# A linear-attention and gated MLP kernel on one core: the weight guard as a later check, the state product in four TensorE tiles, eight masks moved from VectorE

## The chip, the cores and the metric

The kernel runs on one core of one Trainium2 chip. The metric is device time of one execution in microseconds, the median of several runs; before the change it is 392.2 us (three runs, 391.81 to 392.32).

## What is computed

For 4 batches and 8 heads a recurrence over 768 steps runs on states of 48 by 48; its output, with the heads side by side, goes through a token-shifted, gated MLP (384 to 1024 to 384):

```python
f = 1.0 / (1.0 + np.exp(-f_logit))
for t in range(S):
    state = f[:, :, t, :, None] * state + np.einsum('bhd,bhe->bhde', k[:, :, t], v[:, :, t])
    y[:, :, t] = np.einsum('bhd,bhde->bhe', q[:, :, t], state)
...
xk = mu_k * x + (1.0 - mu_k) * x_prev      # x: y with heads joined; x_prev: one step earlier
xr = mu_r * x + (1.0 - mu_r) * x_prev
k = np.maximum(xk @ w_k, 0.0)
v = k * k @ w_v
r = 1.0 / (1.0 + np.exp(-(xr @ w_r)))
return (r * v).astype(np.float32)
```

The weights arrive as 64-bit floats, as pairs of 32-bit words, and are made into 32-bit floats on the chip.

## The kernel before

**Attention.** The work is cut into 24 chunks of 128 steps (six to a batch). Two heads share a tile, head a in partitions 0 to 47 and head b in 64 to 111, and four such pairs make the 8 heads. For chunk i the names of the steps are: b (scan of the gates on VectorE, L203), ln and rb (logarithm and exponential on ScalarE), q, n and k (products on VectorE, L213, L233, L225 and L229), kr (two products on GpSimd, L221 and L222), SC (scores, TensorE, L274, into the PSUM tiles pss0 for heads a and pss1 for heads b), ma and mb (the two masked copies to SBUF, L300), TR and kt (transposed k, L259, and its copy, L262), ZQ (the state's product with q, L284), VV (scores times v, L284), PP (new state contribution, L315, into the PSUM tile pp), zs and z (state update on VectorE, L247 and L249), and y (two ScalarE copies from the PSUM tile py into x and stage, L330). SC uses TensorE as four independent 64 by 64 tiles. ZQ uses it as two: heads a in rows and columns 0 to 63, heads b in the other half. VV uses all 128 rows and alternates between the two column halves.

**MLP.** Three chunks make a unit of 384 steps; there are 8 units. Six small DMAs (spread, L385) move heads 6 and 7 from stage into x's free partitions. The mix makes d (three differences, L395), xm (six, L404), and each xm's high part xh and low part xl (L412 or L413, and GpSimd's L419). Every full-size product is the sum of three matmuls of high and low parts (L427): F (eight tiles with w_k), R (three with w_r), W (three output tiles of two halves each with w_v; W0.01 is the second half of unit 0's first tile). Between F and W stand r, h, kk (ScalarE) and k2l (GpSimd, L465).

**Weights.** Each of 18 pieces (wk0 to wk7 of 384 columns, wr0 to wr3 of 288, wv0 to wv5 of 512) goes through A (absolute value on ScalarE, L543), M (maximum with 2^-15, L546), S (shift, L548), T and X (combining the words, L551 and L554, all VectorE), H (cast to the high part, ScalarE, L557) and L (the rest, GpSimd, L561). M guards S against weights of very small size. The six wv pieces pass through two buffers called words.

**Order.** A planner (Plan.schedule, L73) simulates the queues with costs and due times written into each `pl.add`, and emits every engine's instructions in the order that it finds; each engine then runs its own list in order and waits on semaphores. SP issues all DMAs, in order. If any gate product falls below a bound (flag, L608), the slow path `general` runs at the end; it doesn't run here.

Of the kernel before, what the change touches and what calls it, by code (L numbers as in the profile page):

```python
# [47 lines left out]


class Plan:  # L50
# [22 lines left out]
    def schedule(self, trace=None):  # L73
        free = dict.fromkeys("PVAGQ", 0.0)
        wire = 0.0
# [79 lines left out]
class Rwkv:  # L155


    def __init__(self, nc=None, tc=None):
# [17 lines left out]
    def add_attention(self, pl, i):  # L176
# [104 lines left out]
        first = [None, None]  # L281

        def ymm(g2, j, lhs, rhs, stop):
            m = nc.tensor.matmul(  # L284
                self.py[64 * g2 : 64 * g2 + lhs.shape[1], j], lhs, rhs, start=first[g2] is None, stop=stop,
                skip_group_check=True,
            )
            first[g2] = first[g2] or m

        def zq():  # L290
            for j in range(NP):
                for g2 in (0, 1):
                    ymm(g2, j, self.z_t[i % 2][HALF[g2], j], q()[HALF[g2], j], False)

        if cs > 0:
            pl.add(f"ZQ{i}", at, ("P", 0.87, 0, zq), after=I("z") + I("q") + I("y", i - 1) + I("SC"))
        for g2, m in enumerate("ab"):
# [26 lines left out]
        def y_out(e):  # L324

            for r in (slice(0, D), slice(64, 64 + D)) if cs == 0 else (slice(0, P),):
                for o, i_ in ((self.b("x", u)[r, :, 1 + t0 : 1 + t0 + C], self.py[r, 0:3]),
                              (self.b("stage", u)[r, t0 : t0 + C], self.py[r, 3])):
                    if e is nc.scalar:
                        e.activation(o, i_, AF.Copy, scale=-1.0)  # L330
# [4 lines left out]
        pl.add(f"y{i}", at, ("A", us, 0, lambda: y_out(nc.scalar)), ("V", us, 0, lambda: y_out(nc.vector)),
               after=I("VV"), **({"takes" if c == 0 else "uses": [("x", u), ("stage", u)]}))

    def add_unit(self, pl, u):
# [42 lines left out]
    def spread(self, x, stage, j):  # L381

        for g2 in (0, 1):
            r = 64 * g2
            self.nc.sync.dma_start(x[r + 48 : r + 64, j, 1:], stage[r + 16 * j : r + 16 * j + 16, :])  # L385

    def add_mix(self, pl, u, k0, dst, alone=False):
# [46 lines left out]
        for f in range(NF):  # L434
# [36 lines left out]
        for t in range(UC):  # L471
# [343 lines left out]
```

## Time and profile before

| | |
|---|---|
| runs | 392.20, 392.32, 391.81 us |
| profiled execution | 392.84 us; span from first to last instruction 391.1 us |
| TensorE matmul (PE) busy | 339.2 us, 87% of the span, 3241 instructions |
| VectorE (DVE) busy | 231.2 us, 59%, 429 instructions |
| ScalarE (ACT) busy | 237.1 us, 61%, 458 instructions |
| GpSimd (POOL) busy | 184.6 us, 47%, 212 instructions |
| data moved by DMA | 34.17 MB, mean 87 GB/s |
| mean granted TensorE clock | 0.977 of full speed |

A row of a timeline is start, duration, engine, line, operation, tiles (buffer numbers left out), count, and in brackets the idle time of the engine before it with what ended it. A group row ends with busy time, mean nanoseconds of one, and idle time before the group. PE is the matmul part of TensorE and PEld its weight loads. One fp32 matmul of the attention shows as two PE instructions. Rows of the chain of waits are start, duration and what ran.

### The profile page before, as it was taken

To read this page: it belongs to the slowest core of one execution; us is meant where nothing else is said; L and a number is where in the kernel's file an instruction comes from. 1 tells how busy PE (TensorE), PEld (TensorE's weight loads), DVE (VectorE), ACT (ScalarE), POOL (GpSimd) and SP (SyncE) were. 2 spreads that over 40 slices of the span, in tenths; PEclk is the share of its full clock that TensorE was granted. 3 is DMA by queue.
4 is the path that set the end of the run, shared out by engine and by line. 5 is a ranking of instruction groups with operands and counts; after the bars stand their busy time and mean duration, and the time that the engine had idled before them with its cause. 6 is when DMAs were issued, how large, how long until landed. Compare 5 with 4: busy or idle time off the path is not lost.

```text
span 391.1 us, 8274 instructions
## 1 busy us (share of the span) xinstructions
PE 339.2 (87%) x3241; PEld 314.9 (81%) x3241; DVE 231.2 (59%) x429; ACT 237.1 (61%) x458; POOL 184.6 (47%) x212
## 2 busy tenths in 40 slices
PE   0077227699999999999999999999999999999994
PEld 0066126689898998999899989999899989999993
DVE  6989699998797588318851688049822731161001
ACT  4773348868478765747675655856584436565830
POOL 1451377764667564534574364618361613334600
PEclk9999859999999999999999999999999999999999
DMA  7999611343550243421321123032301100011001
GB/s 250 402 372 233 150 54 55 108 99 84 140 118 5 59 99 108 117 60 38 103 62 33 45 83 102 2 75 76 91 20 30 47 23 2 1 37 40 3 21 47
DMA packets 17918, 34.17 MB, mean 87 GB/s; under 512 B 2928, under 2 KB 13040, under 8 KB 17872
## 3 DMA queue, kind: packets, MB, share of 16 engines
q1 hardware_dynamic: 17872, 33.57, 30.1%
q8 instruction: 27, 0.44, 0.5%
q14 instruction: 19, 0.16, 0.1%
HBM read 27.66 MB, written 4.72 MB: 83 GB/s over the span
## 4 chain that ended last, share of the span: by engine, by line
PE 78%; DVE 9%; DMA 8%; ACT 1%; issue 1%; SPq 1%; DVEq 0%
PE pm L427 59%; PE py L284 10%; PE pss L274 5%; DMA v<-in_vt 3%; PE pm L259 2%; DMA f<-in_zt 2%; DMA x<-stage 2%; PE pp L315 2%; DVE pm L548 1%; DVE pm L551 1%; DVE pm L546 1%; DVE xm L404 1%; DVE pm L395 1%; DMA x<-in_wr 1%; DVE words L554 1%
## 5 line engine op out<-in xcount | busy, mean ns | idle before, releaser
L427 PE MATMUL pm<-xh,wk 128*128 128x384 f32 x384 | 107.5, 350 | 19.1 <-DVE words_k2h L554 13.5
L427 PE MATMUL pm<-wv,k2h 128*128 128x384 f32 x384 | 99.8, 341 | 0.4 <-DVE xm L404 0.4
L465 POOL TENSOR_TENSOR k2l<-kk,k2h 128x384 fp32r<-128x384 f32 x64 | 65.0, 1018 | 60.3 <-ACT kk L459 38.3
L427 PEld LDWEIGHTS pm<-xh,wk 128*128 128x128 f32 x384 | 71.6, 192 | 22.8 <-issue 14.1
L419 POOL TENSOR_TENSOR xl<-xm,xh 128x384 fp32r<-128x384 f32 x48 | 53.3, 1125 | 50.3 <-DVE xh L413 39.7
L427 PEld LDWEIGHTS pm<-wv,k2h 128*128 128x128 f32 x384 | 69.0, 188 | 1.8 <-issue 0.9
L427 PE MATMUL pm<-xl,wk 128*128 128x384 f32 x192 | 65.9, 343 | 0.0
L427 PE MATMUL pm<-wv,k2l 128*128 128x384 f32 x192 | 64.8, 338 | 0.0
L300 DVE TENSOR_TENSOR ss<-pss,cst_sb 128x512 f32<-128x512 f32 x48 | 30.8, 683 | 53.5 <-PE pss L274 53.3
L450 ACT ACTIVATE r<-pm 128x384 f32<-128x384 f32 x64 | 31.4, 490 | 32.2 <-PE pm L427 27.9
L274 PE MATMUL pss<-qk 64*64 64x128 f32 (+1 forms) x768 | 23.1, 258 | 22.1 <-DVE qk L225 22.1
L274 PEld LDWEIGHTS pss<-qk 64*64 64x64 f32 x768 | 19.6, 139 | 27.4 <-DVE qk L225 22.1
L427 PE MATMUL pm<-wr,xh 128*128 128x384 f32 x144 | 38.5, 349 | 0.0
L427 PEld LDWEIGHTS pm<-xl,wk 128*128 128x128 f32 x192 | 36.8, 192 | 0.0
L395 DVE TENSOR_TENSOR pm<-x 128x384 f32<-128x384 f32 x24 | 18.2, 757 | 30.9 <-DMA x<-stage 30.7
L427 PEld LDWEIGHTS pm<-wv,k2l 128*128 128x128 f32 x192 | 36.1, 188 | 0.0
L455 ACT ACTIVATE k2h<-r 128x384 fp32r<-128x384 f32 x64 | 33.6, 525 | 2.0
L517 DVE TENSOR_TENSOR o<-pm,lg 128x384 f32<-128x384 f32 x24 | 13.2, 551 | 35.7 <-PE pm L427 35.7
L221 POOL TENSOR_TENSOR qk<-qk,rb 128x256 f32<-128x256 f32 x24 | 22.5, 937 | 24.5 <-ACT rb L211 14.2
L203 DVE TENSOR_TENSOR_SCAN pm<-f,low 128x512 f32<-128x512 f32 x24 | 32.8, 1365 | 0.0
L412 ACT CAST xh<-xm 128x384 fp32r<-128x384 f32 x36 | 18.2, 514 | 20.2 <-DVE xm L404 20.0
L459 ACT ACTIVATE kk<-r 128x384 f32<-128x384 f32 x59 | 30.0, 509 | 0.1
(81 smaller groups left out, 529.2 us busy)
## 6 DMA issues: line engine op xcount, KB each, us to landing
qk<-in_qkt SPq DMA_DIRECT2D x40, 192.0 KB, 3.4
v<-in_vt SPq DMA_DIRECT2D x24, 192.0 KB, 2.5
out<-o SPq DMA_DIRECT2D x24, 192.0 KB, 1.9
words<-in_wv SPq DMA_DIRECT2D x6, 512.0 KB, 3.7
f<-in_zt SPq DMA_DIRECT2D x10, 288.0 KB, 4.9
qk<-in_qkt SPq DMA_DIRECT2D x4, 512.0 KB, 8.8
f<-in_zt SPq DMA_DIRECT2D x2, 768.0 KB, 8.4
words_k2h<-in_wk SPq DMA_DIRECT2D x4, 384.0 KB, 9.4
```

What stands on the lines that cost most here:

```text
L203: pl.add(f"b{i}", ga, ("V", 1.25, 1, lambda: nc.vector.tensor_tensor_scan(b().rearrange(FL), f().rearrange(FL), self.low.rearrange(FL), 1. ...
L221: e.tensor_tensor(k()[:, ::2], k()[:, ::2], rb()[:, ::2], op=ALU.mult)
L274: nc.tensor.matmul(self.pss[g2][HALF[h ^ j], j0 + j, 64 * h :], k()[HALF[g2], j0 + j, HALF[h ^ j]], q()[HALF[g2], j0 + j, 64 * h :], start ...
L284: m = nc.tensor.matmul(self.py[64 * g2 : 64 * g2 + lhs.shape[1], j], lhs, rhs, start=first[g2] is None, stop=stop, skip_group_check=True,)
L300: nc.vector.tensor_tensor(s4, p4, self.mask.unsqueeze(1).to_broadcast([P, 2, 2, C]), op=ALU.mult)
L395: pl.add(f"d{u}.{j}", pr, ("V", 0.56, 1, lambda j=j: nc.vector.tensor_tensor(pm("d", u, j)[:, :UT], x()[:, j, 1:], x()[:, j, :UT], op=ALU. ...
L419: e.tensor_tensor(lo(), xm(), hi().bitcast(F32), op=ALU.subtract)
L427: nc.tensor.matmul(ps, lhs(a, j), rhs(bb, j), start=ends[0] and i == 0, stop=ends[1] and i == len(pr) - 1)
L450: pl.add(f"r{u}.{f}", kf, ("A", 0.5, 0, lambda r=r, ps=ps: nc.scalar.activation(r(), ps(), AF.Relu)), ("V", 0.56, 0, lambda r=r, ps=ps: nc ...
L455: pl.add(f"h{u}.{f}", kf, ("A", 0.53, 0, lambda r=r, hi=hi: nc.scalar.activation(hi(), r(), AF.Square)), after=[f"r{u}.{f}"], **kw)
L459: ("A", 0.53, 0, lambda r=r, kk=kk: nc.scalar.activation(kk(), r(), AF.Square)),
L465: e.tensor_tensor(lo(), kk(), hi().bitcast(F32), op=ALU.subtract)
```

## The change

Three things are changed together, and with them the planner's numbers and so the order.

1. *Guard as a check.* A and M go from all 18 pieces; S now reads the loaded words. In their place `add_check` loads all weights a second time, in 15 pieces through the two words buffers, and reduces each to its least absolute value (VectorE). The least of all joins the flag. The slow path makes the weights again, with the guard.
2. *State product in four tiles.* ZQ and VV write to two PSUM tiles: even pairs to py, odd pairs to pz, which is the second half of the bank that holds pp. For odd pairs the column halves are swapped, so that ZQ's four matmuls of two pairs use the four 64 by 64 tiles in turn. VV's column halves follow each other as 0 1 1 0 0 1 1 0. y becomes four copies (six in the first chunk of a batch), since the swapped pair must be put back, and is placed after PP.
3. *Masks.* For chunks 0 to 7 mb is a plain ScalarE copy, and GpSimd multiplies by the mask in SBUF (mg); VV waits for it.

```diff
+CHECK = (2.0, 0.2)
+AWAY = [(i, 1) for i in range(8)]
...
             if e == "Q":
-                done = wire = max(wire, start + 1.5) + us
-                free[e] = start + 0.06
+
+                for _ in range(port):
+                    start = max(start, under[-8])
+                    wire = max(wire, start + 1.6) + us / port
+                    under.append(wire + 0.3)
+                    start += 0.45
+                done, free[e] = wire + 0.3, start
...
         def ymm(g2, j, lhs, rhs, stop):
-            m = nc.tensor.matmul(
-                self.py[64 * g2 : 64 * g2 + lhs.shape[1], j], lhs, rhs, start=first[g2] is None, stop=stop,
-                skip_group_check=True,
-            )
+
+            h = g2 ^ j % 2
+            to = (self.pz if j % 2 else self.py)[64 * h : 64 * h + lhs.shape[1], j // 2]
+            m = nc.tensor.matmul(to, lhs, rhs, start=(h, j % 2) not in first, stop=stop, skip_group_check=True)
...
+            if (i, g2) in AWAY:
+                ss = lambda: self.b("ss", (i, 1))
+
+                def by_mask():
+                    s4 = ss().rearrange("p (a b) c -> p a b c", b=2)
+                    nc.gpsimd.tensor_tensor(
+                        s4, s4, self.mask.unsqueeze(1).to_broadcast([P, 2, 2, C]), op=ALU.mult)
+
+                pl.add(f"m{m}{i}", at, ("A", 0.59, 0, lambda: nc.scalar.copy(ss(), self.pss[1])), after=I("SC"),
+                       takes=[("ss", (i, g2))])
+                pl.add(f"mg{i}", at, ("G", 1.35, 0, by_mask), after=I("mb"), uses=[("ss", (i, g2))])
...
-                for o, i_ in ((self.b("x", u)[r, :, 1 + t0 : 1 + t0 + C], self.py[r, 0:3]),
-                              (self.b("stage", u)[r, t0 : t0 + C], self.py[r, 3])):
+                for o, i_ in ((x[r, 0:3:2], self.py[r]), (stage[r], self.pz[r, 1])):
...
+            for r in (0, 64):
+                o, i_ = x[r : r + D, 1], self.pz[64 - r : 64 - r + D, 0]
...
-               after=I("VV"), **({"takes" if c == 0 else "uses": [("x", u), ("stage", u)]}))
+               after=I("VV") + I("PP"), **({"takes" if c == 0 else "uses": [("x", u), ("stage", u)]}))
...
-            pl.add(f"{name}A{p}", place, ("A", us(0.00104, 0.14), 0, lambda: nc.scalar.activation(
-                t(), high().bitcast(F32), AF.Abs)), after=[f"{name}{p}"], takes=[t_key], uses=[home])
             dve = us(0.00104, 0.15)
-            pl.add(f"{name}M{p}", place, ("V", dve, 0, lambda: nc.vector.tensor_scalar(
-                t(), t(), 2.0**-15, None, op0=ALU.max)), after=[f"{name}A{p}"], uses=[t_key])
...
+            pl.add(f"c{p}", CHECK[0] + CHECK[1] * p, ("Q", n * P * 8 / 380e3, 1, lambda v=v, w=w, c=c: nc.sync.dma_start(
+                v(), w.rearrange("p a b t -> p (a b) t")[:, c])), takes=[("words", ("c", p))])
+            pl.add(f"cm{p}", CHECK[0] + CHECK[1] * p + 1, ("V", 0.00104 * n + 0.15, 0, lambda v=v, p=p: nc.vector.tensor_reduce(
+                self.least[:, p : p + 1], v()[..., 1].bitcast(F32), axis=mybir.AxisListType.X, op=ALU.min,
+                apply_absolute_value=True)), uses=[("words", ("c", p))])
...
+            nc.vector.scalar_tensor_tensor(
+                self.flag, m()[:, 1:2], 2.0**-15, m()[:, 0:1], op0=ALU.is_lt, op1=ALU.max)
...
-    k.py = pm.tile([P, NP, C], F32, name="py")
+
+    k.py = pm.tile([P, 512], F32, name="py")[:, : 2 * C].rearrange("p (a c) -> p a c", a=2)
     k.pp = pm.tile([P, 512], F32, name="pp")
+    k.pz = k.pp[:, 256:].rearrange("p (a c) -> p a c", a=2)
```

What it does to the order is seen at three places. The first is VectorE's list (DVE) where unit 0's mix begins. L395 is d, L404 is xm, and L546, L548, L551, L554 are M, S, T, X of a piece. Before:

```order
L554 SCALAR_TENSOR_TENSOR words_k2l_126<-words_k2l_126,pm_88 128x3x128
L395 TENSOR_TENSOR pm_88<-x_101 128x384
L404 SCALAR_TENSOR_TENSOR xm_105<-pm_88,mu_sb,x_101 128x384
L546 TENSOR_SCALAR pm_86<-pm_86 128x384
L548 TENSOR_SCALAR pm_86<-pm_86 128x384
L551 SCALAR_TENSOR_TENSOR pm_86<-words_k2l_126,pm_86 128x384
L554 SCALAR_TENSOR_TENSOR words_k2l_126<-words_k2l_126,pm_86 128x3x128
L395 TENSOR_TENSOR pm_86<-x_101 128x384
```

The same place now, with d at L428, xm at L437 and S, T, X at L578, L587, L590:

```order
L590 SCALAR_TENSOR_TENSOR words_k2l_127<-words_k2l_127,pm_90 128x3x128
L578 TENSOR_SCALAR pm_89<-words_k2h_128 128x384
L428 TENSOR_TENSOR pm_87<-x_102 128x384
L437 SCALAR_TENSOR_TENSOR xm_106<-pm_87,mu_sb,x_102 128x384
L428 TENSOR_TENSOR pm_88<-x_102 128x384
L437 SCALAR_TENSOR_TENSOR xm_107<-pm_88,mu_sb,x_102 128x384
L428 TENSOR_TENSOR pm_90<-x_102 128x384
L437 SCALAR_TENSOR_TENSOR xm_108<-pm_90,mu_sb,x_102 128x384
L437 SCALAR_TENSOR_TENSOR xm_109<-pm_87,mu_sb,x_102 128x384
```

Before, piece wk3 stands between the first and the second d; now wk3 and the shift of wk4 stand ahead of the mix, and the nine instructions of the mix follow each other.

The second place is TensorE's list (PE) where unit 0's W meets chunk 5: k2l_666 ends W0.01, pss is SC, z is ZQ, and k2h_539 begins the second output tile. Before:

```order
L427 MATMUL pm_87<-wv_79,k2l_666 128x384
L274 MATMUL pss_81<-qk_65 64x128
L274 MATMUL pss_82<-qk_65 64x128
...
L274 MATMUL pss_82<-qk_65 64x64
L284 MATMUL py<-qk_65,z_71 64x128 x8
L427 MATMUL pm_86<-wv_79,k2h_539 128x384
```

Now, where k2l_572 ends the first half W0.00, L272 is TR, and k2h_619 begins W0.01:

```order
L460 MATMUL pm_90<-wv_79,k2l_572 128x384
L287 MATMUL pss_81<-qk_65 64x128
...
L300 MATMUL py<-qk_65,z_71 64x128 x2
L300 MATMUL pp<-qk_65,z_71 64x128 x2
...
L272 MATMUL pm_89<-cst_sb,qk_66 128x128 x4
L287 MATMUL pss_81<-qk_66 64x128
...
L460 MATMUL pm_90<-wv_79,k2h_619 128x384
```

SC and ZQ of chunk 5 and TR and SC of chunk 6 moved from behind W0.01 to ahead of it, and ZQ's eight matmuls go to py and to pp's bank by turns.

The third place is VectorE's list at the state update after chunk 1, zs and z, with what each instruction waits for. Before:

```order
L554 SCALAR_TENSOR_TENSOR words_k2h_125<-words_k2h_125,pm_86 128x3x128 [waits DVE_49]
L247 TENSOR_TENSOR pp<-pp,z_71 128x192 [waits PE_49]
L249 TENSOR_TENSOR z_70<-pp,g 128x4x48 [waits DVE_49]
L300 TENSOR_TENSOR ss_93<-pss_81,cst_sb 128x512 [waits PE_49]
L300 TENSOR_TENSOR ss_92<-pss_82,cst_sb 128x512 [waits PE_49]
```

Now:

```order
L242 SCALAR_TENSOR_TENSOR qk_67<-pm_90,qk_67 128x2x64
L260 TENSOR_TENSOR pp<-pp,z_71 128x192 [waits PE_49,Activation_49]
L262 TENSOR_TENSOR z_70<-pp,g 128x4x48 [waits DVE_49]
L578 TENSOR_SCALAR pm_87<-words_k2h_126 128x384 [waits DMAHW2_49]
L587 SCALAR_TENSOR_TENSOR pm_87<-words_k2h_126,pm_87 128x384 [waits DVE_49]
L315 TENSOR_TENSOR ss_95<-pss_81,cst_sb 128x512 [waits PE_49]
```

zs now waits for ScalarE too: for the last copy of y of the chunk before, which reads the bank that pp lies in. Of the two masks only that of heads a is left in VectorE's list.

More of the change, by code (lines that the diff above doesn't have):

```diff
@@ L155 @@
 class Rwkv:
+    wk = wr = wv = None
     def __init__(self, nc=None, tc=None):
@@ L356, in add_unit @@
         else:
-            pl.add(f"f{u}", ga - 0.4 if u >= NFB else -1.5 + 0.1 * u, ("Q", 1.8, 0, load), after=gates)
+            pl.add(f"f{u}", ga - 0.4 if u >= NFB else -1.5 + 0.1 * u, ("Q", 2.07 if u < NFB else 1.55, 1 if u < NFB else 2, load), after=gates)
             if u < NFB:
@@ L365, in add_unit @@
         for j in range(KJ):
-            pl.add(f"sp{u}.{j}", u - PREP - 0.1, ("Q", 0.2, 0, lambda j=j: self.spread(x(), s(), j)), after=ys, uses=[("x", u), ("stage", u)])
+            pl.add(f"sp{u}.{j}", u - PREP - 0.1, ("Q", 0.2, 2, lambda j=j: self.spread(x(), s(), j)), after=ys, uses=[("x", u), ("stage", u)])
         if u % NU == 0:
@@ L440, in ff @@
                 mm3(ps(), lambda a, j: wk_p()[a][:, j, f * P : f * P + P], lambda a, j: sp(0)[a][:, j], range(KJ))
-            pl.add(f"F{u}.{f}", kf, ("P", 1.57, 0, ff), after=chain + [f"xl{u}.0{j}" for j in range(KJ)]
+            pl.add(f"F{u}.{f}", kf, ("P", 1.58, 0, ff), after=chain + [f"xl{u}.0{j}" for j in range(KJ)]
                    + ([] if alone else [f"wkL{f}"]),
@@ L476, in rp @@
                 mm3(ps(), lambda a, j: sp(1)[a][:, j, t * P : t * P + P], lambda a, j: wr_p()[a][:, j], range(KJ))
-            pl.add(f"R{u}.{t}", kr, ("P", 1.57, 0, rp), after=chain + [f"xl{u}.1{j}" for j in range(KJ)]
+            pl.add(f"R{u}.{t}", kr, ("P", 1.58, 0, rp), after=chain + [f"xl{u}.1{j}" for j in range(KJ)]
                    + ([] if alone else [f"wrL{p}" for p in range(4)]),
@@ L592, in add_words, with add_check @@
                   *(lambda c=c, a=a: self.w["wv"][a].rearrange("p a b -> p (a b)")[:, c] for a in (0, 1)), True)
+    def add_check(self, pl):
+        nc = self.nc
+        pieces = [(w, slice(c, c + m)) for w, n, m in ((self.wk, KJ * DFF, 512), (self.wv, NF * DM, 512), (self.wr, KJ * DM, DM))
+                  for c in range(0, n, m)]
+        for p, (w, c) in enumerate(pieces):
+            n = c.stop - c.start
+            v = lambda p=p, n=n: self.b("words", ("c", p))[:, : 2 * n].bitcast(I32).rearrange("p (n t) -> p n t", t=2)
+            pl.add(f"c{p}", CHECK[0] + CHECK[1] * p, ("Q", n * P * 8 / 380e3, 1, lambda v=v, w=w, c=c: nc.sync.dma_start(
[3 more added lines that the diff above has]
+                apply_absolute_value=True)), uses=[("words", ("c", p))])
+        return [f"cm{p}" for p in range(len(pieces))]
@@ L613, in add_start @@
         at = U - 1
[L614 to L620 removed]
+        pl.add("lo", at, ("V", 0.4, 0, least), after=[f"bl{N - 1}"] + self.add_check(pl), takes=[("xm", "lo")])
+        pl.add("lot", at, ("P", 0.2, 0, turn), takes=[("pm", "lo")], uses=[("xm", "lo")])
+        pl.add("lom", at, ("V", 0.6, 0, flag), uses=[("pm", "lo"), ("xm", "lo")])
+        pl.add("strong", at + 0.3, ("Q", 0.0, 0, load), after=["lom"])
     def rows(self, first):
```

139 lines of the change are left out of this document (84 added, 55 removed).

## Prediction

> **What bounds the kernel now.** I read the page first, then busy time by windows, the chain of waits, and the timelines of PE and DVE in the start.
>
> ```profile
> span 391.1 us, 8274 instructions
> PE   0077227699999999999999999999999999999994
> DVE  6989699998797588318851688049822731161001
> ```
>
> PE is full from the ninth slice to the end (a slice is 9.8 us); before that DVE is. By windows (PE, PEld, DVE, ACT, POOL busy, clock, DMA share, GB/s):
>
> ```profile
> 50.00:60.00 10.00, 3.64 (x11) 3.18 (x12) 9.64 (x16) 4.11 (x8) 6.18 (x6) 0.53 0.18 52
> 60.00:70.00 10.00, 7.58 (x41) 6.65 (x40) 9.54 (x17) 9.52 (x22) 8.45 (x8) 1.00 0.30 79
> ...
> 160.00:180.00 20.00, 20.00 (x162) 19.14 (x161) 5.07 (x11) 14.30 (x26) 7.80 (x9) 1.00 0.30 69
> 180.00:200.00 20.00, 20.00 (x227) 18.41 (x226) 17.86 (x32) 11.87 (x27) 12.66 (x15) 1.00 0.28 83
> ```
>
> So there are two regimes. From about 45 to 85 us the DVE queue (weight words, first mix) feeds PE; afterwards PE's own work is the time, and DVE has slack in alternate windows. The joints between them, from the timelines of PE, DVE and SP:
>
> ```profile
> 56.33 0.66 PE L427 MATMUL pm<-xh,wk 128*128 128x384 f32 x1 [13.13 <-DVE words_k2h L554]
> ...
> 90.34 0.52 PE L427 MATMUL pm<-wv,k2h 128*128 128x384 f32 x2
> ```
>
> ```profile
> 38.94 4.67 SPq L385 DMA_DIRECT2D x<-stage  x6
> ```
>
> ```profile
> 44.62 0.57 DVE L395 TENSOR_TENSOR pm<-x 128x384 f32<-128x384 f32 x1 [2.82 <-DMA x<-stage]
> ...
> 45.76 0.56 DVE L546 TENSOR_SCALAR pm<-pm 128x384 f32<-128x384 f32 x1
> ```
>
> The rows are PE's first full-size matmul F and the one at 90.34, SP's issue of the first unit's spread, and the first difference d0 of its mix with the first words step behind it. The row at 90.34 is my marker: W0.01, the second half of unit 0's first output tile, the first work that needs all six wv pieces. Rows of the chain of waits behind it (start, duration):
>
> ```profile
> 92.60 0.83 PE pss L274 x32
> 93.43 0.88 PE py L284 x16
> ...
> 150.90 1.79 PE pm L427 x9
> ...
> 153.52 0.59 PE pm L259 x4
> 154.11 1.02 PE py L284 x16
> ...
> 158.28 11.28 PE pm L427 x63
> ...
> 356.96 28.49 PE pm L427 x162
> ```
>
> PE ends at 356.96 + 28.49 = 385.45; the last product, its store and the close take 391.1 - 385.45 = 5.6. From the marker PE still has 385.45 - 90.34 = 295.1 us.
>
> **The change, part by part.** What happens before 44.62 I leave where it is. SC0, at 22, hangs in the chain on the last early load of f:
>
> ```profile
> 6.75 8.94 DMA f<-in_zt
> ```
>
> The same bytes stand ahead of it, so the abs and the max that go from wr's pieces only lengthen waits there. The first mix waits for the six spread DMAs. Their last input was ready at 35.7 (the first row below), yet SP issued them at 38.94, since it holds each DMA until one eight back has landed:
>
> ```profile
> 35.42 0.27 ACT L330 ACTIVATE stage<-py 128x128 f32<-128x128 f32 x1
> ```
>
> ```profile
> words<-in_wv SPq DMA_DIRECT2D x6, 512.0 KB, 3.7
> ```
>
> The same loads stand ahead of them now. What the change costs here is latency: y grows, and z waits for it (below); two such links of about 0.9 lie before the third y, which moves to about 37.5, still under 38.94. So d0 starts at 44.6 as before. Were that cover gone, each microsecond beyond 38.94 would be one of the total.
>
> *DVE from 44.62 to the last word.* The prices, from one start to the next:
>
> ```profile
> 72.35 1.23 DVE L203 TENSOR_TENSOR_SCAN pm<-f,low 128x512 f32<-128x512 f32 x1
> 73.61 0.69 DVE L213 TENSOR_TENSOR qk<-qk,pm 128x512 f32<-128x512 f32 x1
> 74.22 0.36 DVE L247 TENSOR_TENSOR pp<-pp,z 128x192 f32<-128x192 f32 x1
> ...
> 76.56 0.69 DVE L548 TENSOR_SCALAR pm<-pm 128x512 int32<-128x512 int32 x1
> 77.29 0.70 DVE L551 SCALAR_TENSOR_TENSOR pm<-words,pm 128x512 int32<-128x512 int32 x1
> 77.89 0.42 DVE L225 SCALAR_TENSOR_TENSOR qk<-pm,qk 128x256 f32<-128x256 f32 x1
> 78.23 0.48 DVE L229 SCALAR_TENSOR_TENSOR qk<-pm,qk 128x128 f32<-128x128 f32 x2
> 78.62 0.68 DVE L554 SCALAR_TENSOR_TENSOR words<-words,pm 128x512 int32<-128x512 int32 x1
> ...
> 83.01 0.69 DVE L554 SCALAR_TENSOR_TENSOR words<-words,pm 128x512 int32<-128x512 int32 x1
> ```
>
> A words step of 512 costs 0.73, one of 384 0.60 (0.56 and the same gap); a scan 1.26; q 0.6, and n and a mask, of its size, the same; the k group 0.73; zs and z 0.3 each. The stretch took 83.70 - 44.62 = 39.1. It loses the four max steps of wk4 to wk7 (2.4) and the six of wv (4.4), the mask b of chunk 4 (0.6), and, moved ahead of the mix, wk3's four steps and wk4's shift (3.0): 10.4. The order puts into it the scans of chunks 5 and 6 (2.5), q5, q6, n5, n6 (2.4), k5 (0.7), zs5 and z5 (0.7), mask a of chunk 5 (0.6): 6.9. I add 2.0 for new waits: wv2 to wv5 reuse two buffers, each load waits on SP for the GpSimd subtraction two pieces earlier and takes 3.7 us to land (the row above), and the sixth would be late by about that. The last word is then ready at 44.6 + 39.1 - 10.4 + 6.9 + 2.0 = 82.2. Behind it stand one cast and one subtraction:
>
> ```profile
> L330 ACT ACTIVATE x<-py 128x384 f32<-128x384 f32 (+1 forms) x28 | 13.7, 490 | 22.5 <-PE py L284 22.4
> ...
> L561 POOL TENSOR_TENSOR wv<-words,wv 128x512 fp32r<-128x512 f32 x6 | 8.5, 1410 | 6.2 <-ACT wv L557 6.1
> ...
> L330 ACT ACTIVATE stage<-py 128x128 f32<-128x128 f32 (+1 forms) x28 | 7.5, 267 | 0.0
> ...
> L557 ACT CAST wv<-words 128x512 fp32r<-128x512 f32 x6 | 3.9, 655 | 3.1 <-DVE words L554 3.0
> ```
>
> The first and third rows are today's y. Cast and subtraction give 82.2 + 0.7 + 1.4 = 84.3 for the marker instead of 90.3. PE gets there first: with the mix no longer cut by word steps, its first F starts near 50, not 56.33. Bounds: 82.3 without the new waits; 87.3, half the gain, if GpSimd's waits eat the rest (first rival).
>
> *PE after the marker.* By the order SC5, ZQ5, TR6 and SC6 now stand before W0.01: 0.83 + 0.88 + 0.59 + 0.83 = 3.1 less behind it. Fifteen ZQ follow. Today's run two at a time and take 0.88 to 1.02. No four-tile ZQ is in this trace; the nearest row is SC, which runs four at a time: 16 instructions of 128 columns and 16 of 64, 24 full ones, in 0.83, so 0.035 each; 16 of them make 0.55. I take 0.45 saved, between 0.33 (0.88 - 0.55) and 0.58 (perfect halving twice leaves 0.44 of 1.02): 6.8, bounds 5.0 to 8.7. VV keeps its pairs (two column halves alternate, in the order 0 1 1 0), so its 1.01 stays. The order also has 41 runs of full-size matmuls instead of 46. Nine take 1.79, 63 take 11.28, so one takes 0.176 and each run 0.2 beyond: 1.0 less.
>
> *New waits after the marker.* y was two ACT instructions, 0.49 + 0.27. It is now four, which I price at 0.39 + 0.27 + 0.26 + 0.26 (half-width outputs of 128 columns are nearest to the second row): 0.4 more, and the part in the bank that PP writes waits for PP. In the build zs and z wait for y's last copy, so VV, PP, y, zs, z, ZQ stand in one line where y and z ran side by side. That line is about 0.5 + 0.8 + 0.7 + hand-offs = 2.2 us; behind z on DVE stand masks, n, k and the check's reductions. PE's order has SC, TR and nine F (0.83 + 0.59 + 1.79 = 3.2) or more between a VV and the next ZQ after the start, so most is hidden. The check's 15 reductions (no row has them; bounds 0 and the 0.73 of a 512 step each) fall after the marker, where windows of DVE at 5.07 of 20 hide 11 us; its (3072 + 3072 + 1152) x 8 bytes x 128 = 7.5 MB lie where the DMA share is 0.3. But SP issues in order, and a check load that waits for its buffer holds spreads and q, k loads behind it. Each mask b now costs ACT a copy (like the wv cast, 0.66) and GpSimd 1.4, and VV waits for both, about 1.5 us more than for DVE; the DMA cover before 44.6, and PE's F, R and W between SC and VV of chunks 4 to 7, hide that. I take 2.0 for all this, bounds 0 and 7.
>
> **The sum.** 84.3 + 295.1 - 3.1 - 6.8 - 1.0 + 2.0 = 370.5; with the 5.6 behind, a span of 376.1. The profiled execution took 392.84 for its 391.1, so 1.7 more: 377.9. It stands 0.64 above the median of 392.2; I forecast 377.2.
>
> **Rivals.** *The start gains nothing.* GpSimd has its own queue before the marker:
>
> ```profile
> L465 POOL TENSOR_TENSOR k2l<-kk,k2h 128x384 fp32r<-128x384 f32 x64 | 65.0, 1018 | 60.3 <-ACT kk L459 38.3
> ...
> L419 POOL TENSOR_TENSOR xl<-xm,xh 128x384 fp32r<-128x384 f32 x48 | 53.3, 1125 | 50.3 <-DVE xh L413 39.7
> ```
>
> Six xl (6.7), eight k2l and four wk subtractions (12 x 1.02 = 12.2) and six wv (8.5) make 27.4; three k products of two instructions each (an estimate from 256 of 384 columns: 6 x 0.75 = 4.5) and a mask (1.4) bring it to 33 us from 46 on, so 79 if it never waits. In 50 to 70 it idled 20 - 6.18 - 8.45 = 5.4. If waits keep the marker at 90.3, the time is 377.2 + 6.0 = 383.2. Against it: two feeders of that queue (ACT's abs, DVE's max) are gone.
>
> *ZQ is no faster*: 377.2 + 6.8 = 384.0. For it: only SC shows four tiles at once. Against: the same four 64 by 64 positions, two banks.
>
> *The lengthened line holds PE*, which ends slower. Place: each ZQ after the marker. Price: PE stands w at each of 15. At w = 1.1 all is given back (375.2 + 15 x 1.13 = 392.2); at 1.3, as when one scan stands ahead of zs and uses up the slack each time, 394.7. For it: DVE at 17.86 of 20 in 180 to 200, so z is seldom prompt. Against it: the 3.2 us of cover, and a PE that hardly waited at 90% DVE. The Trainium skill, TensorEngine Tiling (Array Packing), section PSUM Bottleneck, says that tiling speeds up the matmuls but not the emptying of PSUM, which can become the limit; that is this rival, and by it the tiles would give nothing and y's longer copies would set the pace. By that rule, 384 or more; the trace speaks against it: in the two late windows ACT is busy 14.30 and 11.87 of 20.
>
> **How the numbers follow.** Forecast 0.76, start without gain 0.11, ZQ no faster 0.06, line holds PE 0.07 (0.05 beyond the break-even). What counts as different here is 0.2%, 0.8 us. Faster 0.92, same 0.03, slower 0.05. The forecast's own ends: without any new wait and with ZQ at its best 377.2 - 4.0 - 1.9 = 371.3; with the marker at 87.3, the worst waits and ZQ at its least 377.2 + 3.0 + 5.0 + 1.8 = 387.0. The range is 371 to 387, which takes in the first two rivals.
>
> **What would show it.** Right: d0 near 44.6; first F near 50; W0.01 near 84; ZQ near 0.55 in the chain; VV at 1.0; PE idle after the marker near 3 us. Wrong: spreads issued after 39; ZQ near 0.9 or VV above 1.2; PE rows that wait for DVE z or ACT before ZQ; an F that waits for xl behind a check load.

## The result and the profile after

The changed kernel takes 377.5 us (median of four runs, 376.64 to 378.46) against 392.3 for the kernel before (391.81 to 392.74, beside it): a ratio of 0.962, 95% interval 0.959 to 0.965. The forecast was 377.2. The profiled execution took 378.06, with a span of 376.0. Medians and ratios leave out executions more than 1.5% above the fastest of their kernel, which of the changed kernels struck only ZQ in two tiles (three of seven, its profiled one of 391.1 among them, so that only the work behind the marker is read from that profile).

The page of the changed kernel, to be read against the span, the busy times and the PE slices of before:

```profile
span 376.0 us, 8353 instructions
PE 329.1 (88%) x3242; PEld 307.4 (82%) x3242; DVE 217.3 (58%) x400; ACT 249.1 (66%) x517; POOL 197.6 (53%) x220
PE   0076494959999989999999999999999999999994
```

PE's busy time fell from 339.2 to 329.1: that is two thirds of the 15 us. The rest is idle time of PE, nearly all of it ahead of the marker W0.01. The joints between the stages, from the timelines of SP, DVE and PE (start, duration):

```profile
37.20 4.02 SPq L418 DMA_DIRECT2D x<-stage  x6
```

```profile
41.88 0.57 DVE L428 TENSOR_TENSOR pm<-x 128x384 f32<-128x384 f32 x1
...
83.74 0.69 DVE L590 SCALAR_TENSOR_TENSOR words<-words,pm 128x512 int32<-128x512 int32 x1
```

```profile
46.44 0.66 PE L460 MATMUL pm<-xh,wk 128*128 128x384 f32 x1 [4.29 <-ACT xh L445]
...
62.76 0.69 PE L460 MATMUL pm<-xh,wk 128*128 128x384 f32 x1 [5.33 <-ACT r L483]
...
84.82 0.33 PE L272 MATMUL pm<-cst_sb,qk 128*128 128x128 f32 x1 [2.83 <-DVE qk L238]
...
86.58 0.77 PE L460 MATMUL pm<-wv,k2h 128*128 128x384 f32 x2
```

The first d comes at 41.88 (44.62 before), the first F at 46.44 (56.33), the last word at 84.43 (83.70) and the marker W0.01 at 86.58 (90.34). F starts ten microseconds earlier, and then PE stands 5.33 for ScalarE's r. Behind the marker, in the chain of waits, PE ends so:

```profile
326.21 15.83 PE pm L460 x90
342.26 28.20 PE pm L460 x162
370.49 0.56 DVE o L550
```

342.26 + 28.20 = 370.46, so PE has 283.9 us behind the marker (295.1 before). By windows of the changed kernel, VectorE's stretch from the first d to the last word and the one stretch behind the marker in which PE is not full (PE, PEld, DVE, ACT, POOL busy, clock, DMA share, GB/s):

```profile
41.88:84.43 42.55, 28.64 (x251) 25.91 (x247) 37.87 (x60) 32.44 (x65) 33.86 (x34) 0.87 0.38 110
```

```profile
120.00:140.00 20.00, 18.77 (x154) 17.59 (x156) 14.81 (x29) 14.32 (x26) 9.20 (x11) 1.00 0.79 242
160.00:180.00 20.00, 20.00 (x193) 18.82 (x193) 13.33 (x24) 13.18 (x25) 10.37 (x10) 1.00 0.25 78
```

### The profile page after: what moved, and what is told of

It reads as the page before. It is cut to its first block, busy times and chain, and to the rows that moved or that the text cites. A ratio compares the mean times of both kernels' runs of the same rounds, so it can differ in the third digit from the quotient of the medians.

```text
span 376.0 us, 8353 instructions
## 1 busy us (share of the span) xinstructions
PE 329.1 (88%) x3242; PEld 307.4 (82%) x3242; DVE 217.3 (58%) x400; ACT 249.1 (66%) x517; POOL 197.6 (53%) x220
## 4 chain that ended last, share of the span: by engine, by line
PE 77%; DVE 7%; DMA 7%; ACT 4%; issue 2%; SPq 1%; POOL 1%; DVEq 0%; POOLq 0%; ACTq 0%
PE pm L460 59%; PE py L300 6%; PE pss L287 5%; PE pm L272 3%; PE pp L300 3%; DMA f<-in_zt 2%; DMA x<-stage 2%; DMA qk<-in_qkt 1%; PE pp L342 1%; DMA x<-in_wr 1%; DVE pm L587 1%; DVE pm L578 1%; DVE pm L216 1%; SPq L418 1%; DVE words L590 1%
## 5 line engine op out<-in xcount | busy, mean ns | idle before, releaser
L460 PE MATMUL pm<-xh,wk 128*128 128x384 f32 x384 | 106.1, 348 | 9.6 <-ACT r L483 5.3
L498 POOL TENSOR_TENSOR k2l<-kk,k2h 128x384 fp32r<-128x384 f32 x64 | 66.6, 1042 | 55.2 <-ACT kk L492 42.4
L452 POOL TENSOR_TENSOR xl<-xm,xh 128x384 fp32r<-128x384 f32 x48 | 56.6, 1209 | 45.4 <-ACT xh L445 30.0
L315 DVE TENSOR_TENSOR ss<-pss,cst_sb 128x512 f32<-128x512 f32 x40 | 26.1, 682 | 43.4 <-PE pss L287 42.8
L287 PEld LDWEIGHTS pss<-qk 64*64 64x64 f32 x768 | 19.4, 138 | 27.1 <-DVE qk L238 21.5
L216 DVE TENSOR_TENSOR_SCAN pm<-f,low 128x512 f32<-128x512 f32 x24 | 35.2, 1471 | 0.9 <-ACT f L392 0.9
L492 ACT ACTIVATE kk<-r 128x384 f32<-128x384 f32 x64 | 32.6, 509 | 0.0
L445 ACT CAST xh<-xm 128x384 fp32r<-128x384 f32 x45 | 21.7, 512 | 14.8 <-DVE xm L437 14.6
L437 DVE SCALAR_TENSOR_TENSOR xm<-pm,mu_sb,x 128x384 f32<-128x384 f32 x48 | 28.2, 614 | 4.9 <-POOL xl L452 4.0
L460 PEld LDWEIGHTS pm<-wr,xh 128*128 128x128 f32 x144 | 25.1, 188 | 2.6 <-issue 1.1
```

What stands on the lines that cost most here:

```text
L216: pl.add(f"b{i}", ga, ("V", 1.25, 1, lambda: nc.vector.tensor_tensor_scan(b().rearrange(FL), f().rearrange(FL), self.low.rearrange(FL), 1. ...
L287: nc.tensor.matmul(self.pss[g2][HALF[h ^ j], j0 + j, 64 * h :], k()[HALF[g2], j0 + j, HALF[h ^ j]], q()[HALF[g2], j0 + j, 64 * h :], start ...
L315: nc.vector.tensor_tensor(s4, p4, self.mask.unsqueeze(1).to_broadcast([P, 2, 2, C]), op=ALU.mult)
L437: pl.add(f"xm{u}.{n}{j}", pr, ("V", 0.56, 0, lambda xm=xm, n=n, j=j: nc.vector.scalar_tensor_tensor(xm(), pm("d", u, j)[:, :UT], self.mu_s ...
L445: pl.add(f"xh{u}.{n}{j}", pr, ("A", 0.51, 0, lambda xm=xm, hi=hi: nc.scalar.copy(hi(), xm())), ("V", 0.4, 1, lambda xm=xm, hi=hi: nc.vecto ...
L452: e.tensor_tensor(lo(), xm(), hi().bitcast(F32), op=ALU.subtract)
```

## The experiments

Twelve kernels ran. In the table, "against changed" is the difference of the two ratios to the kernel before, times 392.3. Both ratios carry an uncertainty, so that of the difference is 1.6 to 2.2 us to either side (2.7 for the masks). First d and last word are read from VectorE's timeline of the profiled execution; PE's idle time is that from 20 us to its last matmul (25.5 + 0.8 = 26.3 before).

| kernel | median us | ratio (95%) | against changed | first d | last word | PE idle |
|---|---|---|---|---|---|---|
| changed | 377.5 | 0.962 (0.959 to 0.965) | | 41.9 | 84.4 | 21.4 |
| ZQ in two tiles | 384.1 | 0.980 (0.975 to 0.984) | +6.9 | 43.2 | 88.8 | 20.7 |
| max step in 18 pieces | 384.3 | 0.979 (0.976 to 0.982) | +6.6 | 44.0 | 90.1 | 25.2 |
| max step in the first 8 | 379.3 | 0.970 (0.966 to 0.974) | +3.0 | 43.3 | 84.7 | 20.2 |
| before, tiles alone | 387.4 | 0.986 (0.982 to 0.990) | +9.3 | 45.5 | 85.9 | 27.1 |
| PP in py's bank | 379.2 | 0.967 (0.964 to 0.970) | +2.0 | 43.0 | 83.7 | 20.4 |
| no check | 376.0 | 0.957 (0.953 to 0.960) | -2.2 | 41.9 | 82.7 | 17.1 |
| masks back | 377.7 | 0.965 (0.959 to 0.971) | +1.1 | 43.3 | 83.3 | 20.7 |
| old numbers | 387.7 | 0.987 (0.983 to 0.992) | +9.9 | 43.1 | 75.9 | 27.5 |
| scan ahead of GpSimd | 378.3 | 0.964 (0.961 to 0.967) | +0.9 | 42.4 | 82.8 | 18.9 |
| before, new numbers | 404.7 | 1.032 (1.028 to 1.035) | +27.3 | 42.9 | 99.7 | 33.8 |
| late check | 377.4 | 0.962 (0.959 to 0.965) | +0.1 | 42.9 | 83.9 | 18.4 |
| late check, new order | 371.6 | 0.950 (0.947 to 0.952) | -4.9 | 43.5 | 74.7 | 16.3 |

### The four tiles

```diff
-            h = g2 ^ j % 2
+            h = g2
...
-                for g2 in (0, 1):
+                for g2 in ((1, 0) if j % 2 else (0, 1)):
                     ymm(g2, j, self.b("v", i)[:, 2 * j + g2], self.b("ss", (i, g2))[:, j], True)
...
```

The copies of y and the spread, left out here, read the halves where they now lie.

> The changed kernel with its order of instructions kept on every engine, but the state product ZQ in two TensorE tiles again: odd pairs no longer use the swapped column halves. The two PSUM tiles, the four copies of y and the waits between banks stay, and the column halves of VV still follow each other as 0 1 1 0. Theory (the four tiles are what shortens PE's work after the marker W0.01): each of the 15 ZQ behind it takes 0.45 us more, in the chain about 1.0 instead of 0.55, and the time goes from 377.5 to 384.3; the marker stays near 86.6. Rival (the tiles as such give nothing, PE's shorter work comes from the new order): ZQ reads the same and the time stays at 377.5.

Measured: 384.1, or +6.9 us. The rows of PE for one and the same ZQ, first in two tiles, then in four as changed, with the VV that follows:

```profile
147.41 0.44 PE L300 MATMUL py<-qk,z 64*64 64x128 f32 x4
147.68 0.39 PE L300 MATMUL pp<-qk,z 64*64 64x128 f32 x4
147.90 0.39 PE L300 MATMUL py<-qk,z 64*64 64x128 f32 x4
148.12 0.39 PE L300 MATMUL pp<-qk,z 64*64 64x128 f32 x4
148.43 0.43 PE L300 MATMUL py<-ss,v 128*48 128x128 f32 x4
```

```profile
139.83 0.33 PE L300 MATMUL py<-qk,z 64*64 64x128 f32 x2
139.84 0.33 PE L300 MATMUL pp<-qk,z 64*64 64x128 f32 x2
...
140.21 0.28 PE L300 MATMUL py<-qk,z 64*64 64x128 f32 x2
140.22 0.28 PE L300 MATMUL pp<-qk,z 64*64 64x128 f32 x2
140.43 0.43 PE L300 MATMUL py<-ss,v 128*48 128x128 f32 x4
```

In two tiles it takes 148.43 - 147.41 = 1.02, in four 0.60. In four the rows to py and pp start 0.01 apart: they run side by side. Summed from one start to the next over the 15 ZQ behind the marker it is 15.21 against 8.82, 0.43 each and 6.4 in all; another 1.1 is idle time (2.3 against 1.2). The kernel before has the same price for two tiles, 16.19 for 16 ZQ. The theory holds, and the rival that the tiles give nothing falls.

The next kernel is the kernel before with part 2 of the change alone, its order planned anew:

```diff
...
+            to = (self.pz if j % 2 else self.py)[64 * h : 64 * h + lhs.shape[1], j // 2]
...
-               after=I("VV"), **({"takes" if c == 0 else "uses": [("x", u), ("stage", u)]}))
+               after=I("VV") + I("PP"), **({"takes" if c == 0 else "uses": [("x", u), ("stage", u)]}))
...
```

> The kernel before with the second part of the change alone: ZQ and VV into two PSUM tiles, y in four copies after PP; guard, masks and the planner's numbers are those of before, and the planner orders the work anew with ZQ at 0.48 and y at 1.2. Theory: 15 or 16 ZQ behind the marker give 0.45 us each, about 7, and the longer line PP, y, z costs 1 in the start: 392.3 - 7 + 1 = 386.3, between 385 and 388. Rival (z now waits for the last copy of y, and without the other parts VectorE is too full to hide that): the gain is eaten up, 390 to 393.

Measured: 387.4, inside the theory's range; by the ratio that is 5.6 us less than before. PE idles 27.1 us instead of 26.3.

### The guard

```diff
+                else:
+                    nc.vector.tensor_scalar(t(F32), high.bitcast(F32), 2.0**-15, None, op0=ALU.max)
                 nc.vector.tensor_scalar(
                     t(), high, 3, 0x3FFFFFFF, op0=ALU.logical_shift_left, op1=ALU.bitwise_and)
```

> The changed kernel with its order kept, and one more VectorE instruction in each of the 18 pieces of weights: a max step of the size of the removed one, ahead of the shift, whose result is overwritten. ScalarE's abs stays away, the check stays. Theory (VectorE's queue sets the marker): the ten steps behind the first d, four of 0.60 and six of 0.73, add 6.8 us, so the marker goes from 86.6 to 93.4 and the time to 384.3; the first d moves by less than 1 us, since VectorE waits for other engines in a third of the time ahead of it. Rival (GpSimd's queue sets the marker, VectorE has room): marker and time move by 2 us at most, to 379.5. Second rival (VectorE is full ahead of the first d too): the eight steps there come on top, 388 to 389.

Measured: 384.3, as the theory has it, but not for its reason alone. VectorE's timeline of this kernel, first d and last word:

```profile
43.51 0.56 DVE L580 TENSOR_SCALAR pm<-words_k2h 128x384 int32<-128x384 int32 x1
43.98 0.56 DVE L428 TENSOR_TENSOR pm<-x 128x384 f32<-128x384 f32 x1
```

```profile
87.18 0.69 DVE L579 TENSOR_SCALAR pm<-words 128x512 f32<-128x512 f32 x1
...
89.43 0.69 DVE L592 SCALAR_TENSOR_TENSOR words<-words,pm 128x512 int32<-128x512 int32 x1
```

The first d came 2.1 later, the last word 5.7, at 90.12, and the marker 5.9, at 92.5. So VectorE's queue sets the marker, but the ten steps behind the first d lengthened the stretch by 3.6 instead of 6.8, in part since the scan of chunk 4 took 1.23 here (3.47 in the changed kernel, below), and steps ahead of the first d seem to count too. The next kernel holds only the eight steps that lie there (the edit is against the one above):

```diff
-                else:
+                elif name == "wr" or name == "wk" and p < 4:
```

> The changed kernel with its order kept, and the overwritten max step in eight of the 18 pieces alone: wr0 to wr3 and wk0 to wk3, which all lie ahead of the first d. In the run with all 18 the time rose by 6.8 us and the first d came 2.1 us later. Theory of the prediction (ahead of the first d VectorE waits for transfers, so steps there cost nothing): 377.5 to 378.3, the first d at 41.9. Rival (these eight steps lie in the line of the first three chunks' y, and a delay there goes on to the marker): first d 1 to 2 us later, 378.5 to 379.6.

Measured: 379.3, or +3.0 by the ratios (1.8 by the medians), just beyond the uncertainty of 2.0. That speaks for the rival: these eight cost between a quarter and a half of what all 18 cost. The first d at 43.3 says less, since kernels with the same start have it between 41.9 and 42.9 from one execution to the next.

### The longer line behind y

```diff
-    k.pp = pm.tile([P, 512], F32, name="pp")
-    k.pz = k.pp[:, 256:].rearrange("p (a c) -> p a c", a=2)
+    k.pp = bank[:, 256:]
+    k.pz = pm.tile([P, 512], F32, name="pz")[:, : 2 * C].rearrange("p (a c) -> p a c", a=2)
...
```

Here `bank` is py's tile, and the copies of y that read it come first.

> The changed kernel with its order kept, but the state contribution PP in the bank of py instead of that of pz: the state update then waits for the first copy of y alone, not for the last (two copies of 0.26 and one of 0.27 less in the line). Theory (behind the marker PE's other work hides that line, and PE idles only 1.2 us there for another reason): nothing is gained behind the marker; in the start two such links lie ahead of the third y, so the first d comes about 1 us earlier and the time is 376.5 to 377.5. Rival (the line is what holds the rest back): 15 times up to 0.3, and the links of the start, 373 to 375.

Measured: 379.2, no gain; the intervals of the two ratios overlap, and what lies behind a loss of about 2 us wasn't found. The line did get shorter: z of the second chunk starts at 28.61 instead of 29.60. But the first d did not come a microsecond earlier, as the theory had it; it came at 43.0. PE's idle time behind the marker is 1.0 us, against 1.2. So z's wait for y holds nothing there.

### The check

```diff
-            pl.add(f"c{p}", CHECK[0] + CHECK[1] * p, ("Q", n * P * 8 / 380e3, 1, lambda v=v, w=w, c=c: nc.sync.dma_start(
-                v(), w.rearrange("p a b t -> p (a b) t")[:, c])), takes=[("words", ("c", p))])
...
+            pl.add(f"c{p}", CHECK[0] + CHECK[1] * p, ("Q", n * P * 8 / 380e3, 1, lambda: None), takes=[("words", ("c", p))])
...
```

Its reductions are left out in the same way.

> The changed kernel with its order kept, without the check's 15 loads and 15 reductions; it leaves out the guard against very small weights, the least value being set to 1 at the start. Theory: the reductions lie in VectorE's slack; the loads hold back the spread of unit 2, where PE idled 1.2 us (the only idle time behind the marker): 376.3. Rival (the check is hidden altogether, the late spread has another cause): 377.5. Second rival (reductions stand ahead of masks and z and cost more than the idle rows show): 375 or less.

Measured: 376.0, 1.5 less by the medians, 2.2 by the ratios (with an uncertainty of 1.9). Behind the marker PE no longer idles, and it has 282.5 us there instead of 283.9. In the changed kernel the wait was this. First its timeline of DVE, then, with the median time from issue to landing last, the DMA rows of the spread of unit 2 (issued at 126.75) in the changed kernel and in the late check that follows:

```profile
131.31 0.69 DVE L647 TENSOR_REDUCE least<-words 128x1 f32<-128x512 f32 x1 [1.48 <-DMA words<-in_wv]
132.45 0.57 DVE L428 TENSOR_TENSOR pm<-x 128x384 f32<-128x384 f32 x1 [0.46 <-DMA x<-stage]
...
136.50 0.55 DVE L550 TENSOR_TENSOR o<-pm,lg 128x384 f32<-128x384 f32 x1
```

```profile
x<-stage SPq DMA_DIRECT2D x6, 24.0 KB, 4.4
```

```profile
x<-stage SPq DMA_DIRECT2D x6, 24.0 KB, 1.9
```

Beside the check's loads (DMA share 0.79) the spread takes 4.4 us to land instead of 1.9. The first d of unit 2 comes at 132.45, the product o of unit 1 stands behind the mix in VectorE's list, and PE waits 1.23 us for the buffer that o frees. The next kernel keeps the order but moves the check:

```diff
...
+    spots = [f"out{u}.{t}" for u in range(2, 6) for t in (0, 2)] + ["out6.0"]
+    for s, spot in enumerate(spots):
+        here = [f"cm{p}" for p in (2 * s - 2, 2 * s - 1)] + [f"c{p}" for p in (2 * s, 2 * s + 1)]
...
+        at = [x[0] for x in order].index(spot) + 1
+        order[at:at] = [check.pop(n) for n in here if n in check]
...
```

> The changed kernel with the order kept, except for the check: its loads and reductions come later, from the end of unit 2 on, two pieces behind the first and the third output store of each unit, and the least of all just ahead of the flag. Theory (the check's price is its loads beside the spread of units 1 and 2, where PE stood 1.2 us, and its reductions in VectorE's queue beside the words and the second mix): as without the check, 375.5 to 376.5. Rival (the price is the traffic and the reductions wherever they stand): 377.5. Second rival (the reductions or the flag now hold a later unit or the end): 378 or more.

Measured: 377.4, the time of the first rival. PE's idle time behind the marker went, as its window shows:

```profile
120.00:140.00 20.00, 20.00 (x177) 18.97 (x177) 13.24 (x24) 15.18 (x27) 10.20 (x12) 1.00 0.34 87
```

The time did not fall with it: the microsecond that it is worth is about what the intervals can tell. The place of the check explains that stall; what else its absence saves stays open.

### The masks

```diff
-                pl.add(f"m{m}{i}", at, ("A", 0.59, 0, lambda: nc.scalar.copy(ss(), self.pss[1])), after=I("SC"),
+                pl.add(f"m{m}{i}", at, ("A", 0.59, 0, masked), after=I("SC"),
...
```

GpSimd's product is left out.

> The changed kernel with its order kept, the masks of heads b of the first eight chunks back on VectorE in one instruction each, at the place where ScalarE's copy stood; no copy on ScalarE and no product on GpSimd for them. Theory (VectorE is the bound only behind the first d, where one of the eight masks lies before the marker, and another two by it): the time goes up by 0.6 to 1.9 for these, and down by up to 1 since VV of the first chunks waits for a shorter chain: 377 to 379. Rival (the masks carry a good part of the gain of the start): eight times 0.69, 383.

Measured: 377.7, the theory's range. The third part of the change, by itself, gives nothing that these runs can tell, which is to say not more than about 3 us either way.

### The scan beside GpSimd

In the changed kernel's timelines of DVE and POOL, the scan of chunk 4 takes 3.47 us where 1.22 is usual:

```profile
55.82 3.47 DVE L216 TENSOR_TENSOR_SCAN pm<-f,low 128x512 f32<-128x512 f32 x1
```

```profile
54.85 1.10 POOL L597 TENSOR_TENSOR wk<-words_k2l,wk 128x384 fp32r<-128x384 f32 x1
55.85 1.07 POOL L498 TENSOR_TENSOR k2l<-kk,k2h 128x384 fp32r<-128x384 f32 x1
56.83 1.35 POOL L597 TENSOR_TENSOR wv<-words,wv 128x512 fp32r<-128x512 f32 x1
58.08 1.20 POOL L255 TENSOR_TENSOR g<-bl,f 128x4 f32<-128x4 f32 x1
```

GpSimd's three subtractions follow each other without a gap, and behind them g, a product of four columns, takes 1.20 us, until the scan's end at 59.29. It looks as if the scan began only at 58.07, near the end of the last subtraction, and GpSimd then stood in its turn.

```diff
...
+            if pinned and name == "l0.1":
+                self.tc.add_manual_dep(
+                    done[at], scan, mybir.DependencyInfo(mybir.DependencyClass.Sync, mybir.DependencyReason.DATA),
+                    reason="scan first")
```

> The changed kernel with its order kept and one more wait: the GpSimd subtraction of unit 0's second k2l, which ran while VectorE's scan of chunk 4 stood for 3.47 us instead of 1.22, now waits for the end of that scan. Theory (the scan could not begin until GpSimd had nothing to run, and VectorE's queue sets the marker): the scan takes 1.22 to 1.3, begins up to 0.2 later, VectorE's queue is 2 us ahead from there, the stall of 5.33 us of F shrinks to about 3, and the marker comes 2 us earlier: 375.5. Rival (GpSimd's queue, 1.3 us later by this, sets the marker): 377.5 to 378.8. Second rival (the scan is slow for another reason): it still takes 3 us or more and the time stays.

The timelines of DVE and POOL of this kernel:

```profile
56.05 1.23 DVE L216 TENSOR_TENSOR_SCAN pm<-f,low 128x512 f32<-128x512 f32 x1
...
59.81 0.36 DVE L262 TENSOR_TENSOR z<-pp,g 128x192 f32<-128x192 f32 x1 [1.35 <-POOL g L255]
```

```profile
57.36 1.01 POOL L498 TENSOR_TENSOR k2l<-kk,k2h 128x384 fp32r<-128x384 f32 x1 [1.24 <-DVE pm L216]
58.33 1.29 POOL L597 TENSOR_TENSOR wv<-words,wv 128x512 fp32r<-128x512 f32 x1
59.57 0.21 POOL L255 TENSOR_TENSOR g<-bl,f 128x4 f32<-128x4 f32 x1
```

The scan takes 1.23 and g 0.21, which agrees with the supposed mechanism. The profiled execution is 2 us shorter (span 374.0), but its five runs have a median of 378.3: no gain. That is in the range of the first rival, but whether GpSimd's queue holds the marker isn't shown; in the profiled execution it came at 84.9. For one thing z now waits 1.35 for g, behind GpSimd's delayed queue. For another the long wait isn't in every execution, nor is the added wait needed to be rid of it: with the masks back the same scan took 1.23, without the check 1.75, and in the late check 2.00, where the timelines of DVE and POOL read:

```profile
56.74 2.00 DVE L216 TENSOR_TENSOR_SCAN pm<-f,low 128x512 f32<-128x512 f32 x1
```

```profile
56.62 1.03 POOL L597 TENSOR_TENSOR wk<-words_k2l,wk 128x384 fp32r<-128x384 f32 x1
57.61 1.93 POOL L498 TENSOR_TENSOR k2l<-kk,k2h 128x384 fp32r<-128x384 f32 x1
```

Here the scan waited for one subtraction only; the next, close behind it, took 1.93 instead of about 1.02. So 3.47 is the longest of these, and it explains no median.

### The planner's numbers

```diff
-LEAD, GATE, PREP = 1.324, 0.0, 0.992
+LEAD, GATE, PREP = 1.311, 0.0, 0.389
...
-DEAR = {"V": 4.883, "A": 2.568}
+DEAR = {"V": 1.931, "A": 1.198}
```

and WORDS likewise; the other kernel has the opposite edit, in the kernel before.

> The changed kernel with the planner's numbers of before for lead, preparation, the due times of the words and the prices of VectorE and ScalarE (the check's due times and the new costs stay), so with another order. Theory (the gain comes from work removed, the numbers only fit the order to it): 379 to 381, with the loss ahead of the marker and the 283.9 us behind it as they are within 1 us. Rival (the new numbers are the gain of the start): marker back at 90 or later, 381 to 384 or more. Second rival: the numbers do nothing, 377.5.

> The kernel before, its work unchanged, with the changed kernel's numbers for the planner (lead, preparation, due times of the words, prices of VectorE and ScalarE). The changed kernel with the old numbers took 387.7, so the numbers are worth 10 us there. Theory (the numbers fit an order to one set of work and are worth nothing by themselves): not faster than 392.3; since the words then come later in a queue that is longer by 18 max steps, 395 to 402. Rival (the numbers are the better ones for either kernel, and 10 of the 14.8 us are theirs): 383 to 388.

Measured: 387.7 and 404.7, both longer than the theories' ranges; the rival for the first, with a marker at 90 or later, fails as well (80.2). With the other's numbers the changed kernel loses 10 us and the kernel before 12. The rows of PE of the changed kernel with old numbers:

```profile
99.95 0.66 PE L272 MATMUL pm<-cst_sb,qk 128*128 128x128 f32 x4 [2.77 <-DVE o L550]
105.23 0.48 PE L300 MATMUL py<-qk,z 64*64 64x128 f32 x2 [4.62 <-DVE z L262]
...
144.72 0.62 PE L460 MATMUL pm<-wv,k2h 128*128 128x384 f32 x2 [3.88 <-DVE xm L437]
```

Its last word is at 75.9 and its marker W0.01 at 80.2, 8.5 and 6.4 us earlier than in the changed kernel. But the chunks and the second mix were put off for that, and PE stands for them later: 11.9 us behind the marker. With old numbers the changed kernel (387.7) is no faster than the kernel before with the tiles alone (387.4): in that order the guard's removal, the check and the masks together give nothing.

The last kernel has the late check and other numbers, found by trying sets in the planner (LEAD 1.315, PREP 0.955, DEAR 12.631 and 9.882, other WORDS, and chunk 9 for chunk 7 in AWAY).

> The late check, and another set of the planner's numbers, by which the planner itself counts 2.2 us less than by the changed kernel's: lead 1.315, preparation 0.955, other due times and prices, and chunk 9 in place of chunk 7 among the masks of ScalarE and GpSimd. Theory (the planner's count follows the chip only roughly: old numbers were 5.8 worse by its count and 10.2 on the chip): 372 to 378. Rival (the gain of the change rests on its own numbers, any other set loses): 380 or more.

Measured: 371.6, just below the theory's range, by the ratios 4.9 less than the changed kernel, and the fastest of all. The page and the marker in PE's timeline:

```profile
span 368.9 us, 8351 instructions
PE 327.1 (89%) x3242; PEld 306.7 (83%) x3242; DVE 214.0 (58%) x400; ACT 248.5 (67%) x517; POOL 195.8 (53%) x220
```

```profile
79.19 0.51 PE L460 MATMUL pm<-wv,k2h 128*128 128x384 f32 x2
```

Here the marker comes early too, but PE idles only 0.6 us behind it: what was put off isn't missed.

## Why the prediction was right, and where its steps were not

The sum came out, but with two terms off in opposite directions by about 2 us each: the marker came 2.3 late, and behind it PE had 2.3 less than forecast. That they cancelled is luck; the agreement to 0.3 us says nothing for the steps.

*ZQ.* Forecast 0.45 saved in each of 15, measured 0.43, and undoing it gave the time back. Right. VV stayed (0.94 each behind the marker). One bound was misread: 0.58 sets half of 0.88 against 1.02, while half of 1.02 would save 0.51.

*The first d.* "So d0 starts at 44.6 as before" was wrong: 41.88. The step that failed is that SP's hold at 38.94 would stand. In the changed kernel the load eight back, issued at 26.11 instead of 28.06, landed at 36.67 instead of 38.87, and SP issues the spread at 37.20, just behind the third y's copy into stage; that y came when the text said, its last copy at 37.76, near 37.5. Nor is 44.6 tied to the guard: the kernel before with new numbers has its first d at 42.9. That the early steps of wr's pieces "only lengthen waits" is in doubt too: the eight max steps of wr0 to wr3 and wk0 to wk3 cost 1.8 to 3.0 us. No run put wr's alone back, nor ScalarE's abs.

*The stretch.* From first d to last word 39.1 - 10.4 + 6.9 + 2.0 = 37.6 was forecast; the window has 42.55. The list of what leaves and comes was nearly right, but the three scans took 3.47, 1.88 and 1.56 instead of 1.22 each: 3.2 us of standing in this execution. Where the scan of chunk 4 took 1.75 and 2.00 (no check, late check), the stretch still took 40.8 and 41.0. VectorE idled 42.55 - 37.87 = 4.7, against 39.08 - 36.78 = 2.3 before and 2.0 more forecast. One of these waits is the one foreseen for wv's buffers: a wv load issued at 69.19 takes 4.5 to land, and the shift of its piece, at 73.84, came behind an idle time of 1.46. With d 2.7 earlier, the last word came 2.2 later than forecast, and the marker, at 86.58 instead of 84.3, inside its bounds.

*First F* near 50: it came at 46.4 and gained nothing by it, since PE then waited 5.33 us for ScalarE, whose bl, ln and rb of chunk 4 stand behind the long scan. In the other kernels of the same order this wait was 2.2 to 3.8 us.

*Behind the marker* 286.2 was forecast and 283.9 measured. The new waits were priced at 2.0; PE idled 1.2 us there, and 0.8 before. They were not those of the line PP, y, z: a shorter line brought nothing, and the wait was the spread, slowed by the check's loads. The fewer runs of full-size matmuls were undervalued: the sum of these products, from one start to the next, is 228.8 against 229.6, although 12 of them ran at about half speed (below, 1.75 us more) and 0.8 more idle time lies in it. That is 3.3 for six runs (38 instead of 44 behind the marker); if all of it is theirs, which no run shows, it is 0.55 each instead of 0.2.

*Rivals.* "The start gains nothing" came true in part: the marker gained 3.8 of the 6.0 us forecast. But the cause named for it, GpSimd's own queue, showed only as the scans' wait. "ZQ is no faster" and "the lengthened line holds PE" both fell: with y's copies longer, ZQ's gain of 0.43 came through in full. The Trainium skill, TensorEngine Tiling (Array Packing), section PSUM Bottleneck, says that emptying PSUM may become the limit once tiles have sped up the matmuls; in this kernel it did not.

*What the prediction did not see* is how much of the gain rests on the order. It priced the parts with the order as given, which was enough for the time. Put back one by one, in an order planned for them, the parts read: tiles 6.4 to 6.9, the guard's max steps 6.6, the check 1.5 to 2.2 of loss, masks nothing. That adds up to some 11.5 of the 14.8; the rest is open, and ScalarE's abs was put back in no run. With the old numbers the whole change yields only 5.

## What to carry over

A term that is PE's own work, priced from rows that run in the same shape, comes out to a tenth of a microsecond; a term that says when a queue gets through comes out to a few microseconds, since each engine's list is reordered with the change. So look for what an earlier milestone was bought with: a marker 6.4 us earlier went with a kernel 10 us slower, since the work put off for it was missing later. And when work is taken out of a kernel whose order is planned, plan again with several sets of numbers before judging the part.

## What the runs showed of the hardware

- VectorE's scans and GpSimd's instructions stood for each other. Beside a GpSimd queue without gaps the scan of chunk 4 took 3.47 us in the changed kernel, 2.00 in the late check and 1.75 without the check, instead of 1.22; the GpSimd instruction that met it took 1.20 instead of 0.21 (g) and 1.93 instead of 1.02 (k2l). The Trainium skill, SBUF — State Buffer, section SBUF: two separate sides, says that a GpSimd instruction that reads SBUF and a VectorE operation with two SBUF inputs exclude each other from a shared port pair, each for its whole instruction. The rows agree. Which of the two gets the turn where one GpSimd instruction ends and the next begins isn't settled by them: in the late check it was the scan, in the changed kernel's execution two GpSimd instructions went ahead of it.
- After idle times of 1.28 and 2.83 us PE's full-size matmuls ran at half speed. The rows of the chain, behind the marker and in the steady part:

```profile
86.65 3.84 PE pm L460 x12
...
266.23 1.57 PE pm L460 x9
```

  They took 0.32 each against 0.174; the granted clock was 0.55 in the window from 86.58 to 90.40, and 1.00 in that from 82.0 to 86.5. Behind the idle time of 1.28 alone, at 78.4, they had still taken 0.17 each.
- Eight matmuls of 64 by 64 in four tiles and two banks take 0.60 (1.02 in two tiles), near the 0.55 worked out from the scores.
